# Values of one attention unit in a scratch tile, one unit fewer transposed on TensorE, and new leads

## The chip, the cores and the metric

The kernel runs on one core of a Trainium2 chip. The metric is the device time of one execution in microseconds (us). Times from several runs are given as their median; a profiled execution has a time of its own. The engines are TensorE (PE, matmuls, with its weight loads PEld), VectorE (DVE), ScalarE (ACT) and GpSimd (POOL). SyncE (SP) issues all DMAs of this kernel, in program order.

## The reference, cut to what matters

Attention for 4 batches, 8 heads, 576 tokens and head size 64. Heads 0 to 3 see the last 32 tokens ("local"), heads 4 to 7 see the tokens that are a multiple of 32 back ("strided"). Then two feed-forward networks over the 2304 tokens of width 512.

```
scores = where(mask, q @ k.T / 8, -1e9);  attn = softmax(scores);  x = attn @ v
x   = x / sqrt(mean(x*x) + 1e-6) * rms_g
x   = (silu(x @ w_gate) * (x @ w_val)) @ w_out          # 512 -> 1536 -> 512
out = relu(x @ w_in)**2 @ w_out2                        # 512 -> 2048 -> 512
```

All operands are float32, and each product is made of three matmuls of halves (high by high, high by low, low by high).

## The kernel before, in words

**Attention units.** A unit is a pair of heads of one batch; there are 16, in the order of pairs 0, 2, 1, 3 of each batch, so units 0 and 2 are local, 1 and 3 strided, and so on. A unit's steps are: load of q and k (`att_load` "qk", two buffers), scores on PE (`att_qk`, L464 and L476), the maximum (L507, scaled at L508), exponentials with sums on ACT (L524), the reciprocal (L538), the normalization (L545), a transpose of the probabilities, the product on values (`att_pv`, L612), a copy out (L646), and a sum of squares for the norm. The values have a load of their own (`att_load` "v", L439 and L443: one DMA of 384 KB, and for a local unit two more of 96 KB), into a pool of two buffers (`v_p`).

The transpose is done in one of two ways. Units below `NM` (L87, 7) use PE: `att_turn` (L567, small matmuls with an identity) into the two accumulator tiles `first_acc`, where their scores also lie, and `att_keep` copies them to SBUF (L579, ACT or DVE). The later units use a DVE transpose by blocks of 32 (`att_tr`, L553) and a copy of eight SBUF to SBUF DMAs (`att_swap`, L593). When unit `NM - 1` is kept, `done["acc"]` (L768) gives the accumulators' banks to the first output product of block 0. Both ways feed the same `att_pv`.

**Feed-forward.** The first half of network one runs over blocks of 512 tokens (the last has 256), six column tiles each (L1427 to L1429, three matmuls of one product). Block 0 needs the four units of batch 0; its norm is applied after the product, from a row kept in `norm0`, columns 0 to 511 of a scratch tile `fa`; its gates use columns 512 to 1535 (`tmp_slot`), and the weights' conversion uses columns from 1536. The weights come packed in pairs of matrices (1 MB, L1140) through two staging buffers and are converted on DVE, ACT and POOL (L1181 to L1222), as many steps as a unit of attention. The rest of network one and network two (L1912, L2318) are a scheme of seven products per eight.

**What sets the order.** A planner runs when the program is built: every piece of work is a task with a due time and steps; a step names its engine or engines, a cost, a condition and the times that it must wait for. `advance` (L357) takes, again and again, the engine that can start earliest, and on it the step with the smallest due time among those that can start within a small tolerance. So each engine's instructions stand in the planner's order, and an engine in the program never passes a waiting instruction by. The due time of an attention step is that of its unit less `PRI` of the step (the maximum: less `MXP`); the units of batch 0 are due at -50 + u, the others `ATT_LEAD` tiles before their block, the norm `PREP_LEAD` before it. `D_COST` is added to what a DVE step seems to end at before `D_BUSY` us. `PV_AHEAD` is how many units the scores may be ahead of the products on values. All loads wait for their buffer by `take` and `rel`; the values' load is a task of one step, due half a tile after its unit.

**Fillers.** While PE would be idle before block 0, `fill` (L2479) issues matmuls on a blank tile, whose results nobody reads.

Of the kernel before, what the change touches and what calls it, by code (L numbers as in the profile page):

```python
# [8 lines left out]
F32 = mybir.dt.float32  # L9
# [32 lines left out]
VW = LT * 2 * D  # L42
VM = LT // 2 * 2 * D
# [9 lines left out]
WST = 2  # L53

RING = 9

ATT_LEAD, ATT_STEP = 5.322, 0
PREP_LEAD = 6.258
W_LEAD = 0
X_LEAD = 4.164  # L60
WARM0 = 10

HOP = 0.15
# [12 lines left out]
N_QK, N_PV = {"loc": 160, "str": 96}, {"loc": 144, "str": 88}  # L76
QK0, PV0 = {"loc": 1.0, "str": 0.9}, {"loc": 1.25, "str": 0.9}

PRI = {"qk": -3.7, "mask": 12.1, "mx": -12.4, "exp": -0.1, "eps": -0.5, "sum": 15.6, "norm": -1.1, "turn": 3.4, "keep": 12.1, "tr": -1.6,
       "swap": -2, "pv": -2.7, "out": -1.4, "sq": -3, "ms0": 9.4, "add": -1.3}  # L80
MXP, LOADF, BIAS = 8.164, 0.752, 0.972

D_BUSY, D_COST, D_LATE, D_COST2 = 138.427, 1.084, 371.203, 0.648
PV_AHEAD = 5


NM = 7  # L87

ORDER0 = (0, 2, 1, 3)

# [17 lines left out]
    ("P1", 0, 0, "A", None), ("P5", 3, 1, "D", None), ("P6", 4, 2, "A", "s1"), ("P2", 1, 3, "C", "s1"),  # L108
    ("P7", 5, 4, "A", "u2"), ("P3", 6, 5, "D", "s5"), ("P4", 2, 6, "A", "c22"),
]  # L110
W2_LEAD, X2_LEAD, L2_LEAD = 9.789, -0.326, 6.418
X3_LEAD, O_LEAD, H_LEAD = 2.563, -0.69, -0.441
O_ORDER = [(0, 0), (0, 1), (1, 0), (1, 1), (0, 2), (1, 2), (0, 3), (1, 3)]
O_ORDER += [(3, 0)] + [(2, j) for j in range(4)] + [(3, j) for j in range(1, 4)]
O_ORDER += [(p, j) for p in range(4, 7) for j in range(4)]
W3_LEAD, LOADF2, BIAS2, TOL2 = 16.583, 0.334, 1.147, 0
X2_PRI = -1.337


def segments(t0, n):  # L120
# [107 lines left out]
def kernel(ctx: ExitStack, tc: tile.TileContext, loc, strd, w1, w2, g, cst, out):  # L228
# [13 lines left out]
    fa = qa[:, QKB * QKW:]  # L242
# [31 lines left out]
    v_p = pool("v", 2, early)  # L274
# [39 lines left out]
    rel = {k: deque([0.0] * caps[k]) for k in live}  # L314
    order = {}

    def room(k, n=1):
        return live[k] + n <= caps[k]

    def take(k):  # L320
        live[k] += 1
        return rel[k].popleft()

    def give(k, t):
        live[k] -= 1
        rel[k].append(t)

    def in_turn(kind, n):
        return order.get(kind, 0) == n
# [80 lines left out]
    first_acc, warming, ms0, first_in = [], [True], [], []  # L410

    def kind(u):
        return "loc" if units[u][1] < 2 else "str"
# [9 lines left out]
    def att_load(u, what):  # L423
        b, p = units[u]
        src = (loc if p < 2 else strd)[b, p % 2]
        w = QW[kind(u)] + KW[kind(u)]
        if what == "qk":
            o = QKW * turn_of("qk", QKB)
            t = qa[:, o:o + QKW]
            if p < 2:  # L430
                nc.sync.dma_start(out=t[:, :w], in_=src[:, :w])
            else:
                nc.sync.dma_start(
                    out=t[:, :2 * SL].rearrange("p (e c) -> p e c", e=2),
                    in_=src[:, :w].rearrange("p (e c) -> p e c", e=2)[:, :, :SL],
                )
        else:
            t = v_p.tile([128, VW + VM], F32, tag="v", name="v")
            nc.sync.dma_start(out=t[:, :VW], in_=src[:, w:w + VW])  # L439
            if p < 2:  # L440
                mid = src[32:96, w:w + VW].rearrange("p (k a n) -> p a k n", a=2, n=2 * D)
                for a in range(2):
                    nc.sync.dma_start(  # L443
                        out=t[64 * a:64 * a + 64, VW:].rearrange("p (k n) -> p k n", n=2 * D), in_=mid[:, a]
                    )
        qkv[what, u] = t
# [6 lines left out]
    def att_qk(u):  # L453
# [3 lines left out]
        masked = u < NM2  # L457
        if u < NM:
            sc = [first_acc[u % 2][:, h] for h in range(2)]
# [220 lines left out]
    def att_task(u, due):  # L680
# [5 lines left out]

        def load(what):
            def f(_, t):
                take(what)
                att_load(u, what)  # L690
                done[what, u] = lanes.dma(
                    QL[kd] + KL[kd] if what == "qk" else VW + (VM if kd == "loc" else 0), t,
                    3 if what == "v" and kd == "loc" else 1, 600,
                )
                turn("load" + what)
            return f
# [27 lines left out]
        def exp(i0, i1):  # L724
            def f(_, t):
# [3 lines left out]
                if NM <= u < NM2:  # L729
                    for h in range(2):  # L730
                        if i0 < nt * (h + 1) <= i1:
                            give("s", t)
            return (None, [[("A", 0.33 * (i1 - i0))]], f, None, due - PRI["exp"])

# [36 lines left out]
        def pv(_, t):  # L771
            take("s")
            take("s")
            att_pv(u)
            qkv.pop(("v", u))
            give("v", t)
            give("pt", t)
            turn("pv")

# [35 lines left out]
        def step(k, ok, alts, fn, when=None):  # L815
            return ok, alts, fn, when, due - PRI[k]

# [4 lines left out]
        if u < NM:  # L822
            steps += [
                (
                    lambda: in_turn("qk", u) and (u < 2 or ("sc", u - 2) in done), [[("T", QK0[kd] + 0.5, N_QK[kd] + 4)]], qk,
                    lambda: max(done["qk", u], done.get(("sc", u - 2), 5.3)), due - 10 - PRI["qk"],
                ),
# [53 lines left out]
        if not alone:  # L881
# [1 line left out]
            steps.append(step("add", None, [dvx(m)] if b == 0 else [dvx(m), gps(m)], add))  # L883
        tasks.append(Task(due, steps))
        tasks.append(Task(due + 0.5, [
            (lambda: room("v") and in_turn("loadv", u), [[("Q", 0.0)]], load("v"), lambda: rel["v"][0])
        ]))


# [225 lines left out]
    wst, wt, raws = {}, {}, []  # L1115
    slots_w = [None] * RING
    mats = [
# [1274 lines left out]
    for i in range(NB):  # L2392
        if i == 0:
            tasks.extend(split_tasks(
                (0, 0), -44, BLOCKS[0][1], lambda k: [(0, xr[0][:, k, 0:BLOCKS[0][1]])], got="xo"
            ))
        prep_task(i, at[0, i, 0] - PREP_LEAD if i else -45)
        if i >= LOADED:
            load_task(i, at[0, i, 0] - X_LEAD)
    for ph in NJS:  # L2400
# [63 lines left out]
    with tc.manual_schedule():  # L2464
# [19 lines left out]
        def next_load(due):  # L2484
# [4 lines left out]
            out=ms0[0], lhsT=blank[:, 0:1].to_broadcast([128, 128]), rhs=blank[:, 0:1].to_broadcast([128, 512]),  # L2489
# [113 lines left out]
```

## Time and profile before

| | us |
|---|---|
| runs of the kernel before (3) | 886.64, 888.31, 888.44; median 888.31 |
| profiled execution, its own time | 888.45 |
| its span, first to last instruction | 886.7 |
| around the span | 1.75 |
| PE busy | 873.9 (99%) |
| DVE busy | 651.2 (73%) |
| ACT busy | 443.7 (50%) |

The profile lists instructions with their start and duration from the span's first instruction. Matmuls are pipelined, so one that lasts 0.39 us can start 0.23 us after the one before; their records count every pass. A timeline row is start, duration, engine, line, operation, output<-input, shape, count, and in brackets the idle time of the engine before it with what ended it. "issue" is time in which the engine waited for nothing that the profile shows.

### The profile page before, as it was taken

To read this page: it belongs to the slowest core of one execution; us is meant where nothing else is said; L and a number is where in the kernel's file an instruction comes from. 1 tells how busy PE (TensorE), PEld (TensorE's weight loads), DVE (VectorE), ACT (ScalarE), POOL (GpSimd) and SP (SyncE) were. 2 spreads that over 40 slices of the span, in tenths; PEclk is the share of its full clock that TensorE was granted. 3 is DMA by queue.
4 is the path that set the end of the run, shared out by engine and by line. 5 is a ranking of instruction groups with operands and counts; after the bars stand their busy time and mean duration, and the time that the engine had idled before them with its cause. 6 is when DMAs were issued, how large, how long until landed. Compare 5 with 4: busy or idle time off the path is not lost.

```text
span 886.7 us, 17216 instructions
## 1 busy us (share of the span) xinstructions
PE 873.9 (99%) x6777; PEld 817.3 (92%) x6782; DVE 651.2 (73%) x1104; ACT 443.7 (50%) x1141; POOL 72.1 (8%) x66
## 2 busy tenths in 40 slices
PE   8999999999999999999999999999999999999998
PEld 5778778878888999999999999999999999999998
DVE  5998977978889776967965876868875456548466
ACT  5986866422312243434533556656565375364462
POOL 0210620100100000000100100001000003002002
PEclk9999999999999999999999999999999999999999
DMA  9865563676794995494498998876699989949714
GB/s 347 268 214 190 181 209 83 217 240 226 237 370 147 372 409 226 154 374 157 166 334 330 384 408 336 334 265 241 275 309 336 365 318 379 307 166 353 239 37 178
DMA packets 77586, 236.79 MB, mean 267 GB/s; under 512 B 7489, under 2 KB 29761, under 8 KB 71617
## 3 DMA queue, kind: packets, MB, share of 16 engines
q1 hardware_dynamic: 77504, 235.70, 73.4%
q8 instruction: 53, 0.87, 0.4%
q14 instruction: 29, 0.23, 0.1%
HBM read 151.91 MB, written 80.48 MB: 262 GB/s over the span
## 4 chain that ended last, share of the span: by engine, by line
PE 81%; DMA 10%; DVE 7%; issue 1%; ACT 1%; SPq 0%; DVEq 0%; ACTq 0%
PE a L1912 14%; PE pg L1912 7%; PE pb L1912 7%; PE gv L1427 6%; PE a L1427 5%; PE gv L1429 5%; PE a L1429 5%; PE a L1428 5%; PE gv L1428 5%; PE a L2318 5%; DMA wst_a<-in_w 5%; PE pg L2318 3%; DMA wi_d<-wst_a 2%; PE pb L2318 2%; DMA wf_d<-wst_a 2%; PE xo L612 1%
## 5 line engine op out<-in xcount | busy, mean ns | idle before, releaser
L1912 PE MATMUL a<-ra 128*128 128x384 f32 x912 | 173.4, 335 | 0.9 <-DVE fb L1960 0.6
L1912 PEld LDWEIGHTS a<-ra 128*128 128x128 f32 x912 | 159.7, 188 | 2.0 <-DVE fb L1960 0.9
L1427 PE MATMUL gv<-ra 128*128 128x512 f32 (+1 forms) x240 | 90.9, 379 | 0.0
L1429 PE MATMUL gv<-ra 128*128 128x512 f32 (+1 forms) x240 | 88.5, 369 | 0.1
L1428 PE MATMUL gv<-ra 128*128 128x512 f32 (+1 forms) x240 | 88.4, 369 | 0.0
L1912 PE MATMUL pg<-ra 128*128 128x384 f32 x426 | 83.6, 336 | 1.1 <-DVE fb L1960 1.0
L1912 PE MATMUL pb<-ra 128*128 128x384 f32 x426 | 83.0, 335 | 0.4 <-DVE fb L1960 0.4
L1912 PEld LDWEIGHTS pg<-ra 128*128 128x128 f32 x426 | 74.7, 188 | 2.1 <-DVE fb L1960 2.1
L1912 PEld LDWEIGHTS pb<-ra 128*128 128x128 f32 x426 | 74.8, 188 | 0.7 <-DVE fb L1960 0.7
L1366 DVE TENSOR_TENSOR wst_a<-fa,wst_a 128x512 fp32r<-128x512 f32 (+1 forms) x76 | 48.0, 633 | 22.0 <-ACT wst_a L1330 19.0
L1427 PEld LDWEIGHTS gv<-ra 128*128 128x128 f32 x240 | 45.2, 189 | 8.1 <-issue 0.3
L1429 PEld LDWEIGHTS gv<-ra 128*128 128x128 f32 x240 | 45.3, 189 | 7.8
L1428 PEld LDWEIGHTS gv<-ra 128*128 128x128 f32 x240 | 45.3, 189 | 6.9
L1330 ACT ACTIVATE wst_a<-fa 128x512 fp32r<-128x512 f32 (+1 forms) x59 | 33.9, 576 | 31.0 <-DMA wi_d<-wst_a 19.5
L1429 PE MATMUL a<-ra,rb 128*128 128x384 f32 x144 | 48.4, 336 | 0.0
L1427 PE MATMUL a<-ra,rb 128*128 128x384 f32 x144 | 48.4, 336 | 0.0
L1428 PE MATMUL a<-ra,rb 128*128 128x384 f32 x144 | 48.4, 336 | 0.0
L1427 PE MATMUL a<-ra 128*128 128x512 f32 (+1 forms) x120 | 45.6, 380 | 0.9 <-ACT pt L579 0.9
L1429 PE MATMUL a<-ra 128*128 128x512 f32 (+1 forms) x120 | 44.9, 375 | 0.0
L1428 PE MATMUL a<-ra 128*128 128x512 f32 (+1 forms) x120 | 44.8, 374 | 0.0
L1199 DVE SCALAR_TENSOR_TENSOR fa<-wst_a,fa 128x1024 int32<-128x1024 int32 x34 | 41.6, 1224 | 1.0
L1514 ACT ACTIVATE fa<-gv 128x512 f32<-128x512 f32 (+1 forms) x18 | 9.5, 527 | 65.4 <-PE gv L1429 65.4
(259 smaller groups left out, 1918.7 us busy)
## 6 DMA issues: line engine op xcount, KB each, us to landing
wst_a<-in_w SPq DMA_DIRECT2D x34, 1024.0 KB, 6.2
ra<-wi_d SPq DMA_DIRECT2D x18, 1792.0 KB, 10.6
wi_d<-wst_a SPq DMA_DIRECT2D x42, 512.0 KB, 4.0
rb<-wf_d SPq DMA_DIRECT2D x16, 1024.0 KB, 7.9
xf_d<-ra SPq DMA_DIRECT2D x21, 768.0 KB, 5.0
ra<-xf_d SPq DMA_DIRECT2D x21, 768.0 KB, 7.4
wo_d<-wst_a SPq DMA_DIRECT2D x14, 512.0 KB, 8.3
wf_d<-wst_a SPq DMA_DIRECT2D x28, 256.0 KB, 6.5
```

The lines of the kernel that those rows point to most:

```text
L612: nc.tensor.matmul(out=o, lhsT=v, rhs=rhs, start=True, stop=True)
L1199: nc.vector.scalar_tensor_tensor(out=bits(), in0=word(1), scalar=-0x40000000, in1=bits(), op0=ALU.bitwise_and, op1=ALU.bitwise_or)
L1330: nc.scalar.activation(out=dst, in_=by_form(raw(a, b)), func=ACTF.Copy)
L1366: eng.tensor_tensor(out=x[:, :, 1], in0=by_form(raw(a, b)), in1=x[:, :, 0].bitcast(F32), op=ALU.subtract)
L1427: nc.tensor.matmul(out=o, lhsT=whi, rhs=x_hi, start=first, stop=False)
L1428: nc.tensor.matmul(out=o, lhsT=whi, rhs=x_lo, start=False, stop=False)
L1429: nc.tensor.matmul(out=o, lhsT=wlo, rhs=x_hi, start=False, stop=last)
L1514: nc.scalar.activation(out=tile_t()[:, :n], in_=ps[:, :n], func=ACTF.Silu)
L1912: nc.tensor.matmul(out=o, lhsT=l, rhs=v, start=need is None and k + n == 0, stop=k == 1 and n == 2, skip_group_check=need is not None,)
L2318: nc.tensor.matmul(out=c[role, m]["ap"][:, :SN], lhsT=l, rhs=v, start=need is None and first and i == 0, stop=last and i == 2, skip_group_ ...
```

## The change

Unit 2 (the third) gets columns 0 to 1151 of the scratch tile `fa` for its values instead of a buffer of `v_p`; its load then has no buffer to wait for, and its product gives none back. `NM` goes from 7 to 6, so unit 6 is transposed by DVE and DMAs, and its scores go to the `s` banks. Leads, priorities and the planner's cost of DVE get other values, and `PV_AHEAD` goes from 5 to 6.

```diff
-ATT_LEAD, ATT_STEP = 5.322, 0
-PREP_LEAD = 6.258
+V_APART = 2
+
+ATT_LEAD, ATT_STEP = 5.891, 0.063
+PREP_LEAD = 7.496
 W_LEAD = 0
-X_LEAD = 4.164
+X_LEAD = 3.422
...
-PRI = {"qk": -3.7, "mask": 12.1, "mx": -12.4, "exp": -0.1, "eps": -0.5, "sum": 15.6, "norm": -1.1, "turn": 3.4, "keep": 12.1, "tr": -1.6,
-       "swap": -2, "pv": -2.7, "out": -1.4, "sq": -3, "ms0": 9.4, "add": -1.3}
-MXP, LOADF, BIAS = 8.164, 0.752, 0.972
-
-D_BUSY, D_COST, D_LATE, D_COST2 = 138.427, 1.084, 371.203, 0.648
-PV_AHEAD = 5
-
-
-NM = 7
+PRI = {"qk": -4.9, "mask": 15.2, "mx": -7.3, "exp": 0, "eps": -0.2, "sum": 10.8, "norm": -0.6, "turn": 2.2, "keep": 11.4, "tr": -3.1,
+       "swap": -4.1, "pv": -0.2, "out": 1.5, "sq": -4.8, "ms0": 10.3, "add": 0.4}
+MXP, LOADF, BIAS = 2.974, 0.752, 1.006
+
+D_BUSY, D_COST, D_LATE, D_COST2 = 143.605, 1.407, 343.785, 0.648
+PV_AHEAD = 6
+
+
+NM = 6
...
-W2_LEAD, X2_LEAD, L2_LEAD = 9.789, -0.326, 6.418
-X3_LEAD, O_LEAD, H_LEAD = 2.563, -0.69, -0.441
+W2_LEAD, X2_LEAD, L2_LEAD = 8.99, -0.326, 6.418
+X3_LEAD, O_LEAD, H_LEAD = 3.503, -1.055, -0.697
...
-W3_LEAD, LOADF2, BIAS2, TOL2 = 16.583, 0.334, 1.147, 0
-X2_PRI = -1.337
+W3_LEAD, LOADF2, BIAS2, TOL2 = 16.305, 0.334, 1.147, 0
+X2_PRI = -0.95
...
-            t = v_p.tile([128, VW + VM], F32, tag="v", name="v")
+            t = fa[:, 0:VW + VM] if u == V_APART else v_p.tile([128, VW + VM], F32, tag="v", name="v")
...
-                take(what)
+                if what == "qk" or u != V_APART:
+                    take(what)
...
-            give("v", t)
+            if u != V_APART:
+                give("v", t)
...
-            (lambda: room("v") and in_turn("loadv", u), [[("Q", 0.0)]], load("v"), lambda: rel["v"][0])
+            (
+                lambda: (u == V_APART or room("v")) and in_turn("loadv", u), [[("Q", 0.0)]], load("v"),
+                None if u == V_APART else lambda: rel["v"][0],
+            )
```

## Rows read from the trace of the kernel before

**Rows 1.** The page, part 1: busy time, share of the span, instructions.

```profile
PE 873.9 (99%) x6777; PEld 817.3 (92%) x6782; DVE 651.2 (73%) x1104; ACT 443.7 (50%) x1141; POOL 72.1 (8%) x66
```

**Rows 2.** Stretches: length, busy time by engine, granted PE clock, DMA share, GB/s.

```profile
0.00:20.00 20.00, 16.78 (x362) 10.06 (x366) 11.32 (x19) 10.79 (x52) 0.34 (x6) 1.00 0.94 343
20.00:40.00 20.00, 19.06 (x476) 15.10 (x474) 19.14 (x29) 18.89 (x84) 3.56 (x2) 0.91 0.84 273
...
80.00:280.00 200.00, 198.41 (x1810) 162.58 (x1797) 167.32 (x291) 88.68 (x305) 30.87 (x26) 0.99 0.64 214
280.00:880.00 600.00, 597.59 (x3488) 594.73 (x3488) 416.58 (x711) 293.79 (x584) 33.45 (x29) 1.00 0.77 286
```

**Rows 3.** Groups of PE by line, 0 to 75 us: the fillers.

```profile
L2479 PE MATMUL warm<-blank 128*128 128x512 bf16 x35 | 11.1, 475 | 1.6 <-DVE blank L2470 0.9 <-issue 0.7
...
L2479 PE MATMUL ms<-blank 128*128 128x512 bf16 x7 | 1.9, 381 | 0.2 <-issue 0.2
```

**Rows 4.** The chain of waits in order of time, 0 to 80 us.

```profile
9.70 9.46 DMA wst_a<-in_w
...
33.52 0.83 DVE nm L507
...
34.77 0.14 DVE ri L538
```

**Rows 5.** PE's waits over the whole span: total, times, longest.

```profile
PE xo L612 <- issue: 1.6, 1, 1.6
...
PE a L1427 <- ACT pt L579: 0.9, 1, 0.9
...
PE xo L612 <- DMA pt<-tr: 0.7, 2, 0.4
```

**Rows 6.** Timeline of PE: unit 2's product, unit 6's turn, the first output product.

```profile
30.34 1.54 PE L612 MATMUL xo<-pt,v 64*64 64x32 f32 x72
...
59.68 1.32 PE L567 MATMUL a<-cst_sb,sm 64*64 64x64 f32 x37
...
62.62 0.50 PE L1427 MATMUL a<-ra 128*128 128x512 f32 x1 [0.87 <-ACT pt L579]
```

**Rows 7.** Timelines of ACT and DVE: unit 5's copy, unit 6's normalization.

```profile
56.85 0.87 ACT L579 ACTIVATE pt<-a 128x384 f32<-128x384 f32 x2 [0.20 <-PE a L567]
...
58.48 0.83 DVE L545 TENSOR_TENSOR sm<-sm,ri 128x640 f32<-128x640 f32 x1
```

**Rows 8.** The tile of the later units' transposes, whole span: durations min/median/max in ns.

```profile
L593 SPq DMA_DIRECT2D pt<-tr x72: 507/590/1687, 83.5 to 205.7; - x72
L553 DVE STREAM_TRANSPOSE tr<-sm x9: 835/922/973, 82.5 to 181.2; 128x768 f32<-128x768 f32 x5, 128x640 f32<-128x640 f32 x4
...
DMA to landing us min/median/max: 1.8/2.7/9.5
```

**Rows 9.** Timeline of SP: the loads of the values of units 1 and 2.

```profile
5.23 0.45 SPq L439 DMA_DIRECT2D v<-in_strd  x1
...
20.12 0.34 SPq L439 DMA_DIRECT2D v<-in_loc  x1
```

**Rows 10.** Two stretches of the start, columns as in rows 2.

```profile
2.00:10.00 8.00, 7.84 (x146) 4.46 (x146) 2.04 (x4) 2.27 (x13) 0.00 (x0) 1.00 1.00 379
10.00:19.00 9.00, 7.57 (x203) 4.88 (x201) 8.76 (x15) 6.43 (x40) 0.00 (x0) 1.00 1.05 377
```

**Rows 11.** Timelines of SP and PE, 185 to 198 us: a late copy.

```profile
185.24 9.84 SPq L593 DMA_DIRECT2D pt<-tr  x8
...
194.53 0.39 PE L1429 MATMUL gv<-ra 128*128 128x512 f32 x1
...
197.54 0.50 PE L1427 MATMUL a<-ra 128*128 128x512 f32 x1
```

**Rows 12.** Two stretches behind it, columns as in rows 2.

```profile
195.00:200.00 5.00, 4.25 (x79) 3.54 (x80) 4.09 (x7) 1.62 (x6) 0.00 (x0) 0.80 0.73 170
200.00:205.00 5.00, 5.00 (x21) 4.06 (x20) 2.65 (x4) 0.50 (x2) 0.00 (x0) 0.86 0.78 274
```

## The prediction

> **What bounds the kernel now.** I read the busy line of the page first. TensorE (PE) is busy 99% of the span, VectorE (DVE) 73%, ScalarE (ACT) 50% [rows 1]: no other engine can bound the whole, so time goes only where PE stops, runs slowly, or does work that the result doesn't need. The table of stretches says where [rows 2]. From 80 to 880 us PE is idle 1.6 + 2.4 = 4.0 us out of 800. The first 20 us hold 3.2 idle us, the next 20 hold 0.9. So the feed-forward phases are a stream of matmuls at a fixed rate, and an edit to the attention's order can win little there.
>
> The start is another matter, and its busy digits mislead: the groups of the filler matmuls (on a blank tile, issued where PE would wait) hold 11.1 + 1.9 = 13.0 us [rows 3]. With the idle 4.1 us some 17 us of the first 41 are not work. In that stretch DVE is busy 19.1 us and ACT 18.9 of 20 [rows 2]: they, and the loads before them, set the moment at which block 0 streams. The chain of waits shows this: the load of the second weight pair (9.46 us until 19.16), then ACT and DVE one after the other on it, DVE's maximum of unit 4, the reciprocal of unit 3, and so on to PE [rows 4].
>
> Last, PE's waits past the start: 0.87 us before the first output product at 62.62, on ScalarE's copy of unit 6's turned probabilities, and 0.7 us on the late copy of a transposed tile near 195 [rows 5].
>
> **The sum is made against the profiled execution**: 888.45 us, its span 886.7 and 1.75 around it. That is 0.14 above the median of the runs, 888.31.
>
> **The change, part by part.**
>
> *Unit 6 leaves TensorE's transpose (NM 7 to 6).* Removed are its 40 small matmul records on PE: 37 in 1.32 us, the last three among the next product's [rows 6]. These lie in the in-order PE stream, so they go one for one: -1.3. Unit 6 also frees the accumulator banks: they now become free after unit 5's copy, at about 57.7 [rows 7], and the first output product has no copy to wait for. I let the 0.87 us go as well. Next in PE's order there is unit 5's product on values, right behind the turn, whose copy of 57.7 is long done; PE stays fed. Added: one DVE transpose of 128x640, 0.835 to 0.97 us, and a copy of eight DMAs, 0.51 to 0.59 us of SP each (4.1 to 4.7), landing 2.7 us later by the median, 9.5 at worst [rows 8]. Two ACT copies go in exchange, like unit 5's pair of 0.87 us [rows 7]. None of this is on PE; from 59.3, where unit 6's normalization ends [rows 7], 0.9 + 4.7 + 2.7 is 67.6, 5 us behind the first output product [rows 6], which is the cover: twelve such matmuls and those of block 0's next tile stand in PE's order there. If it fails, PE waits for the copy, by up to 6.8 us more with the worst landing. I take 0; the upper bound is the price of the one late copy that the trace has, +2.8 (worked out under B), the lower 0.
>
> *Unit 2's values go to the scratch tile.* Its step loses the only thing it waited for, the product of unit 0. Now SP issues it at 20.12, when that product is done [rows 9]. After the change its turn comes right behind the values of unit 1 (5.23) [rows 9], so its 576 KB (384 and twice 96) stand before the qk loads of units 2 and 3 and before the second weight pair (9.70 [rows 4]). At the 377 to 379 GB/s that DMA moved from 2 to 19 us, with all 16 engines busy, this is 589,824 / 378e3 = 1.6 us [rows 10]. The four loads behind it land up to 1.6 us later, and the second pair is on the chain [rows 4]. Against it: SP no longer stands before that load until 20.1, and 576 KB are gone from the stretch after 20. But unit 2's product ran at 30.34 [rows 6], 10 us after the load was issued, and PE's waits before products on values are on instruction issue and on late copies, on no load of values [rows 5]. So I see no direct gain in it. The columns are first reused for block 0's norm and gates, which stand behind all four products of the first batch on PE, unit 2's among them: no new wait. Values of units 3 and 4 may also be loaded one product earlier; neither was waited for. Bounds 0 to +1.6, taken +0.8: half, since DVE and ACT have attention work that can be put before the weights.
>
> The Trainium skill, "DMA: Bandwidth & Descriptors", section on queues, rings and completion order, says that each DMA engine consumes the descriptors of a ring in ring order. This speaks against moving a load forward on SP's one busy queue; the trace agrees in that the second weight load, with the loads issued before it still in flight, stood on the chain for 9.46 us [rows 4]. That page's specifications also limit HBM to about 358 GB/s for a core, by which the 576 KB would be 1.65 us and the term +0.83 in place of +0.8; the row is above that limit, and the row is used.
>
> *Priorities and leads.* The maximum's lead falls from 8.16 to 2.97. Today DVE does unit 4's maximum and its scaling at 33.52, before the reciprocal of unit 3 at 34.77, and the chain runs through both [rows 4]: behind it the maximum would cost unit 3 nothing, so the step wins 0 to 1.25 us. Taken: -0.8, nearer to the whole, since the chain has no other engine between the two. DVE work is made dearer in the first 143 us, attention and the block's preparation are due earlier, the second phase's weights later. These change which of several ready steps goes first on an in-order queue. No row prices them; the nearest are the single waits of about 0.8 us [rows 5]. Bounds: one such wait less or two more, -0.8 to +1.6; I take 0, since PE has 4.0 idle us in the 800 that follow and DVE is busy only 167 of 200 from 80 to 280 [rows 2], so that there is little to win and cover to lose.
>
> Sum: -1.3 - 0.87 + 0.8 - 0.8 = -2.2 us, so 886.3 in the profiled execution and **886.1** by the median.
>
> **Rivals.**
>
> *B: the late copy goes too.* At 185.24 the eight DMAs of one unit's transpose take 9.84 us on SP behind a weight store; its product on values then runs in pieces, from 194.9 to 197.5, 2.6 us where unit 2's took 1.54 [rows 6, 11], and the granted clock is 0.80 and 0.86 in the next two stretches of 5 us (part of them at 1.2 instead of 2.4 GHz): 1.1 + 5 x 0.34 = 2.8 us [rows 12]. The new leads move that unit against the store. If they meet no more and nothing like it comes, 886.1 - 2.8 = 883.3. For it: one of nine copies was hit, all others passed. Against: 10 copies now, with the same stores.
>
> *C: the start pays.* The value load delays the second weights by its full 1.6 us, and the maximum's move wins nothing (ACT is as full as DVE there, and would be next). Then -2.2 + 0.8 + 0.8 = -0.6, 887.7: no change that can be measured. By the Trainium skill's ring order (page and section as above) the delay would be whole.
>
> *D: slower, by late copies.* The place is SP's queue between 60 and 210 us, where each transposed unit issues eight DMAs in a row; earlier leads put them beside weight stores and loads. The price is the 2.8 us of the one seen. One more leaves +0.6; from two more on it decides: -2.2 + 5.6 = +3.4, 891.7. For it: there is one copy more, and SP took up to 9.84 us for eight [rows 11]. Against: 8 of 9 cost PE nothing.
>
> **How the numbers follow.** A measurement of this kernel tells about 0.2%, 1.8 us, from no change: faster is below 886.5, slower above 890.1. Forecast 0.36, B 0.21, C 0.25, D 0.18. The forecast stands just under the line, so of its 0.36 I count 0.26 as faster and 0.10 as the same; C is the same, but for 0.02 on either side; B is faster, with 0.01 left as the same; D is slower. Faster 0.48, same 0.32, slower 0.20. The likeliest case alone runs from 884.0, with its three open terms at their lower ends, to 887.7, where it becomes C. The range takes in B with 0.8 us below it, and of D the case of a single late copy beside a start that pays (886.1 + 2.8 + 1.6 = 890.5): 882.5 to 890.5.
>
> **What would show it.** Right: six units' turns on PE, the last near 55, and no wait on the copy before the first output product, which comes some 2 us before 62.62; ten transposes on DVE. The value load of unit 2 on SP before 8 us; the second weights landing between 19.2 and 20.8; the reciprocal of unit 3 no longer behind unit 4's maximum; fillers and idle of the first 41 us still near 17. Busy PE down by 1.3 us less what the fillers change. Wrong: fillers shorter or longer by over 2 us (the start then decides, not unit 6); a new wait of PE on a copy or on DVE between 60 and 280 with a granted clock below 1; or the wait at 195 gone, which would make it B.

## The result, and the profile after

The change makes the kernel slower: median 893.87 us (892.89 to 894.71, 4 runs) against 887.66 for the kernel before on the same chip (886.64 to 888.44, 4 runs), a ratio of 1.0061 with a 95% interval of 1.0042 to 1.0079. Timed again (the run "after_again" below), it was 894.62 against 888.21 (1.0078, 1.0063 to 1.0093). The forecast was 886.1 and its range ended at 890.5: its sign was wrong, and the time lies outside the range. The profiled execution took 894.71, its span 892.9. Its busy times, to set beside [rows 1]:

```profile
PE 874.6 (98%) x6736; PEld 818.9 (92%) x6741; DVE 652.0 (73%) x1097; ACT 444.4 (50%) x1141; POOL 80.6 (9%) x72
```

TensorE's busy time is the same to 0.7 us, and 41 records are gone: the 40 of unit 6's turn, as forecast, and one filler (a matmul on the blank tile). So the 6 us are time in which PE waits, or runs at the lower clock. Stretches of the changed kernel, to set beside [rows 2, 10, 12]:

```profile
20.00:40.00 20.00, 15.61 (x384) 12.41 (x381) 14.46 (x22) 14.88 (x67) 0.00 (x0) 0.75 0.73 246
20.00:25.00 5.00, 1.17 (x32) 1.04 (x28) 2.88 (x5) 2.35 (x15) 0.00 (x0) 0.50 0.82 323
...
80.00:280.00 200.00, 197.06 (x1885) 161.47 (x1884) 167.32 (x283) 90.10 (x318) 33.85 (x29) 0.98 0.64 217
105.00:110.00 5.00, 3.19 (x94) 2.66 (x93) 5.00 (x8) 4.02 (x18) 2.10 (x1) 0.84 0.25 95
110.00:115.00 5.00, 4.97 (x17) 4.42 (x18) 4.29 (x9) 5.00 (x27) 3.61 (x4) 0.50 0.95 344
205.00:210.00 5.00, 3.89 (x82) 3.35 (x82) 3.53 (x6) 1.63 (x6) 0.00 (x0) 1.00 0.71 172
```

From 20 to 40 us PE is busy 15.6 us and was busy 19.1; from 80 to 280 it idles 2.9 us and idled 1.6. Two holes stand out, one at 20 to 25, one at 105 to 115, each with a granted clock down to 0.50 (1.2 in place of 2.4 GHz) behind or in it. The late copy of [rows 11] is still there, 10 us later: its eight DMAs again take 10 us on SP, and the product runs in pieces from 205.4 to 208.0. Only the clock stays at 1.00 behind it, where the kernel before had 0.80 and 0.86 [rows 12]. SP, then PE:

```profile
195.26 10.20 SPq L594 DMA_DIRECT2D pt<-tr  x8
...
205.44 0.30 PE L613 MATMUL xo<-pt,v 64*64 64x32 f32 x4 [0.41 <-DMA pt<-tr]
```

PE's waits name the holes (beside [rows 5]):

```profile
PE xo L613 <- issue: 3.8, 1, 3.8
PE a L477 <- DMA fa<-in_loc: 1.7, 1, 1.7
PE a L1433 <- ACT pt L580: 1.5, 1, 1.5
PE xo L613 <- DMA pt<-tr: 1.1, 3, 0.4
PE bc L928 <- POOL inv L919: 1.0, 1, 1.0
...
PE sc L477 <- DVE inv L912: 0.8, 1, 0.8
```

To see when the time is lost I followed the n-th matmul of the feed-forward through the records of both kernels, and summed PE's gaps and the fillers (matmuls on the blank tile) up to it:

| n-th feed-forward matmul | before: start, gaps + fillers | after | after_again |
|---|---|---|---|
| 4th (block 0 starts) | 41.12, 16.4 | 45.45, 20.2 | 44.57, 19.5 |
| 97th | 76.52, 17.4 | 81.53, 22.4 | 80.68, 21.7 |
| 253rd | 124.75, 18.1 | 134.88, 24.2 | 133.38, 24.9 |
| 541st (all attention done) | 204.72, 18.9 | 213.50, 25.3 | 212.10, 26.0 |
| 4356th, the last | 882.67, 21.3 | 889.00, 26.3 | 888.05, 27.4 |

Some 3.5 to 4.3 us are lost before block 0 starts, another 4.5 or 3.9 by the 541st, and 2.0 to 2.4 come back after it (PE's gaps there are 1.4 and 1.0 us shorter in all than before). At the 97th the two kernels have not done the same work: unit 6's product on values (1.25 us) stands at 65.59 in the kernel before and at 84.35, behind the 97th, in the changed one. At the other four marks the products are level. For equal work the changed kernel loses 1.9 (in after_again 2.0) us from the 4th to the 97th, 3.9 (3.2) from there to the 253rd, and wins back 1.3 from there to the 541st. The first of these stretches holds a longer wait for a copy (1.53 us for 0.87) and a granted clock of 0.66 from 50 to 55 us; no experiment takes it apart.

**The first hole.** The loads on SP, changed kernel (start, duration, line):

```profile
5.67 0.44 SPq L440 DMA_DIRECT2D v<-in_strd  x1
6.16 0.44 SPq L440 DMA_DIRECT2D fa<-in_loc  x1
7.53 3.19 SPq L444 DMA_DIRECT2D fa<-in_loc  x2
11.74 0.33 SPq L432 DMA_DIRECT2D fa<-in_loc  x1
...
13.17 2.87 SPq L1146 DMA_DIRECT2D wst_a<-in_w  x2
```

and in the kernel before:

```profile
7.48 0.33 SPq L431 DMA_DIRECT2D fa<-in_loc  x1
8.92 0.38 SPq L433 DMA_DIRECT2D fa<-in_strd  x1
9.70 6.22 SPq L1140 DMA_DIRECT2D wst_a<-in_w  x2
```

Unit 2's values (L440 and L444 into `fa`) stand where the forecast put them, but unit 2's q and k go out at 11.74 and not at 7.48, the second weight pair at 13.17 and not at 9.70: 3.5 to 4.3 us later, where the forecast said 1.6 at most. SP itself waits:

```profile
SPq L444 <- DMA wst_a<-in_w: 2.0, 1, 2.0
```

The DMA records carry eight completion semaphores in turn, and a DMA's record waits until the one eight places before it has landed. The first weight pair is fourth on SP, so the twelfth DMA waits for its landing (at 10.09; the twelfth is issued at 10.11); the change makes the last of unit 2's three DMAs the twelfth, and all that follows stands behind it. Now the chain of waits (beside [rows 4]) runs through these loads:

```profile
2.63 9.02 DMA v<-in_loc
11.74 6.13 DMA fa<-in_loc
...
18.95 1.29 PE xo L613 x64
20.23 3.83 issue
24.06 0.44 PE xo L613 x8
```

PE gets unit 2's scores at 17.91, 1.9 us later than before, and then stops for 3.83 us in the middle of unit 0's product, where nothing that the profile shows is awaited. Before, the same place cost 1.6 [rows 5]. In this pause lies a block of 16 KB on a DMA queue of kind "instruction". The DMA queues, 17 to 18 us of the kernel before:

```profile
q8 instruction: 1, 0.02, 6.8%
```

and 21 to 22 us of the changed kernel:

```profile
q8 instruction: 1, 0.02, 6.9%
```

I read this as PE waiting for its own code; no run moved the code to try it. By the records that packet starts 0.3 us behind the product before the change (17.25 against 16.97) and 2.7 us after it (21.60 against 18.88), and in all eighteen traces PE goes on 2.3 to 2.8 us after the packet starts. The Trainium skill, "Runtime: NRT & Kernel Launch", section on instruction fetch mechanics, says that code is refilled in blocks of 16 KiB and that the cost is mostly hidden; the trace agrees on the size, and on "mostly": of the eight such packets in the first 60 us of the changed kernel seven go with no such pause. The eighth costs 3.8 us on PE's path, and 1.6 before the change.

**The second hole.** PE, changed kernel, at block 1's norm:

```profile
105.62 1.17 PE L906 MATMUL msb<-ones,ssq 128*128 128x1 f32 x10
...
107.81 1.18 PE L477 MATMUL sc<-fa 64*32 64x64 f32 x78 [0.79 <-DVE inv L912]
110.03 2.36 PE L928 MATMUL bc<-cst_sb,inv 128*128 128x64 f32 x10 [1.05 <-POOL inv L919]
```

DVE and then POOL in the same stretch:

```profile
101.12 1.64 DVE L1540 TENSOR_TENSOR ra<-fa,ra 128x512 fp32r<-128x512 f32 x1
...
105.86 1.22 DVE L1205 SCALAR_TENSOR_TENSOR fa<-wst_a,fa 128x1024 int32<-128x1024 int32 x1
...
107.60 0.15 DVE L912 TENSOR_SCALAR inv<-msb 128x5 f32<-128x5 f32 x1
107.67 1.21 DVE L1210 SCALAR_TENSOR_TENSOR fa<-wst_a,fa 128x1024 int32<-128x1024 int32 x1
```

```profile
100.69 1.52 POOL L546 TENSOR_TENSOR sm<-sm,ri 128x640 f32<-128x640 f32 x1 [2.21 <-DVE ri L539]
107.83 2.10 POOL L919 TENSOR_TENSOR inv<-inv,half 128x5 f32<-128x5 f32 x1 [5.62 <-DVE inv L912]
```

The row sums are ready at 106.8, but DVE is full (busy 5.00 of 5) and does the norm step only at 107.60; POOL's power takes 2.10 us. DVE's L1540 takes 1.64 us where its like takes 0.69, beside a POOL instruction.

### The profile page after: what moved, and what is told of

Same layout as the page of the kernel before. It is cut to its first block, busy times and chain, and to the rows that moved or that the text cites. A ratio compares the mean times of both kernels' runs of the same rounds, so it can differ in the third digit from the quotient of the medians.

```text
span 892.9 us, 17136 instructions
## 1 busy us (share of the span) xinstructions
PE 874.6 (98%) x6736; PEld 818.9 (92%) x6741; DVE 652.0 (73%) x1097; ACT 444.4 (50%) x1141; POOL 80.6 (9%) x72
## 4 chain that ended last, share of the span: by engine, by line
PE 88%; DVE 5%; DMA 5%; issue 1%; SPq 1%; ACT 0%; POOL 0%; DVEq 0%; ACTq 0%
PE a L1918 16%; PE pg L1918 9%; PE pb L1918 8%; PE a L2324 7%; PE a L1433 6%; PE a L1435 6%; PE a L1434 6%; PE gv L1433 5%; PE gv L1435 5%; PE gv L1434 5%; PE pb L2324 2%; PE pg L2324 2%; PE pb L1435 2%; PE pb L1433 2%; PE pb L1434 2%; PE pg L1435 2%
## 5 line engine op out<-in xcount | busy, mean ns | idle before, releaser
L1918 PE MATMUL a<-ra 128*128 128x384 f32 x858 | 160.4, 335 | 0.3 <-ACT a L1955 0.3
L1918 PEld LDWEIGHTS a<-ra 128*128 128x128 f32 x858 | 150.1, 188 | 0.9 <-ACT a L1955 0.6
L1918 PE MATMUL pg<-ra 128*128 128x384 f32 x480 | 94.1, 336 | 0.7 <-DVE fb L1966 0.7
L1918 PEld LDWEIGHTS pg<-ra 128*128 128x128 f32 x480 | 84.4, 188 | 1.1 <-DVE fb L1966 1.0
L1372 DVE TENSOR_TENSOR wst_a<-fa,wst_a 128x512 fp32r<-128x512 f32 (+1 forms) x76 | 48.0, 633 | 19.2 <-ACT wst_a L1336 16.4
L1336 ACT ACTIVATE wst_a<-fa 128x512 fp32r<-128x512 f32 (+1 forms) x55 | 31.7, 577 | 33.3 <-DMA wi_d<-wst_a 21.1
L1205 DVE SCALAR_TENSOR_TENSOR fa<-wst_a,fa 128x1024 int32<-128x1024 int32 x34 | 42.7, 1256 | 0.9
L1210 DVE SCALAR_TENSOR_TENSOR fa<-wst_a,fa 128x1024 int32<-128x1024 int32 x34 | 42.5, 1250 | 0.7
```

The source lines that it names most:

```text
L1205: nc.vector.scalar_tensor_tensor(out=bits(), in0=word(1), scalar=-0x40000000, in1=bits(), op0=ALU.bitwise_and, op1=ALU.bitwise_or)
L1210: nc.vector.scalar_tensor_tensor(out=bits(), in0=word(0), scalar=29, in1=bits(), op0=ALU.logical_shift_right, op1=ALU.bitwise_or)
L1336: nc.scalar.activation(out=dst, in_=by_form(raw(a, b)), func=ACTF.Copy)
L1372: eng.tensor_tensor(out=x[:, :, 1], in0=by_form(raw(a, b)), in1=x[:, :, 0].bitcast(F32), op=ALU.subtract)
L1918: nc.tensor.matmul(out=o, lhsT=l, rhs=v, start=need is None and k + n == 0, stop=k == 1 and n == 2, skip_group_check=need is not None,)
```

## The experiments

Ratios are against the kernel before on the same chip, with 95% intervals. Where nothing else is said, every engine's order but for the edited instructions is that of the kernel named.

**1. after_defer**: the changed kernel, unit 2's three value DMAs behind the third weight load.

```diff
+            if u == V_APART:
+                held.append(issue)
+            else:
+                issue()
...
+        if n == 2:
+            held.pop()()
```

> The changed kernel with one thing moved: the three DMAs of unit 2's values stand on SP behind the third weight load instead of ahead of the loads of units 2 and 3 (every other instruction keeps its place on its engine). Theory S (the early values load delays the start: in the changed kernel the q and k load of unit 2 left SP at 11.74 instead of 7.48 and the second weights landed at 22.0 instead of 19.2): the start comes back, 886 to 889 us, q and k of unit 2 issued near 7.5, no stall of 3.8 us on issue in the first product on values. Theory L (the new leads and priorities give the engines a worse order): it stays at 892 to 895 us, whatever SP does.

Measured: 892.48, ratio 1.0042 (1.0018 to 1.0066). Unit 2's q and k go out at 7.45, the second weights at 9.54, PE's pause shrinks from 3.8 to 1.9 us; the 97th feed-forward matmul starts at 76.65, 0.13 behind the kernel before where the changed kernel was 5.0 behind (in both of these unit 6's product is still to come). Block 0 starts 2.2 us later than before, since a second pause of that kind, 1.8 us, comes at 30.9. From the 97th to the 253rd matmul 3.1 us are lost for equal work all the same. So the rows of the start are as theory S said, and the time, not told apart from that of the changed kernel, lies in theory L's range: the start is one loss, and the second hole another that doesn't hang on it.

**2. before_early**: the kernel before, its plan untouched, unit 2's values in the scratch tile and issued behind unit 1's.

```diff
+            if u == 1:
+                b2, p2 = units[2]
+                v_issue(fa[:, 0:VW + VM], loc[b2, p2 % 2], QW["loc"] + KW["loc"], p2)
```

> The kernel before with its plan unchanged on every engine; only unit 2's values go to the scratch tile, and their three DMAs stand on SP right behind the values of unit 1. Theory S: the whole loss appears without any new lead, 892 to 895 us, and q and k of unit 2 leave SP near 11.7. Theory L: the load costs at most its bytes, 0 to 1.6 us, so 887.5 to 889.5 us.

Measured: 891.91, ratio 1.0032 (1.0011 to 1.0053). The move alone makes the kernel before slower by about 2.8 us: unit 2's q and k at 12.36, a pause for code of 4.0 us, block 0 starts 4.4 us later, and granted clock 0.66 and 0.65 from 20 to 30 us. This is the changed kernel's first loss without its leads; in the time it lies between the two theories.

**3. before_nm6, after_no_apart, before_leads**: one part alone, or all but one, planned anew: six units on PE (an edit to the kernel before); all but the scratch tile; all new constants with seven units and no scratch tile (both edits to the changed kernel).

```diff
-NM = 7
+NM = 6
```

```diff
-V_APART = 2
+V_APART = -1
```

```diff
-V_APART = 2
+V_APART = -1
...
-NM = 6
+NM = 7
```

> The kernel before with NM 6 alone, planned anew with the old leads. The prediction's first step (unit 6's turn and the wait on its copy gone, 2.2 us) says 885.0 to 886.5 us. Its rival, that the order around it changes and gives the gain back in new waits of PE, says 887 to 890 us. Neither S nor L touches this run.

> The changed kernel with unit 2's values back in the ring of two buffers (V_APART -1), planned anew with the new leads and NM 6. Theory S: 885 to 889 us, since the start's loads are as before and the turn of unit 6 is saved. Theory L: 892 us or more.

> The leads and priorities alone: the kernel before with all new constants, seven units on TensorE and unit 2's values in the ring. The prediction's reading (the constants only choose among ready steps): -0.8 to +1.6 us against the kernel before. Rival: a set of constants fits one plan only, as the other parts alone showed (+2.6% for six units, +4.45% without the scratch tile): more than 1% slower, by waits on weights and on DVE between 60 and 280 us.

Measured: before_nm6 1.0261 (1.0240 to 1.0282), after_no_apart 1.0445 (1.0421 to 1.0470), before_leads 1.0185 (1.0160 to 1.0209). PE's longest wait in each of the three, in this order:

```profile
PE a L2318 <- DMA rb<-wf_d: 15.2, 1, 15.2
```

```profile
PE pg L2324 <- DMA rb<-wf_d: 15.8, 1, 15.8
```

```profile
PE a L568 <- DVE sm L546: 4.1, 3, 3.0
```

In before_nm6 the first output product stands at 60.48, 2.14 us ahead of the 62.62 of [rows 6] (what that is made of is told below). Then the planner's order comes out differently, and a weight tile is waited for by 15.2 us, until 752; before_leads waits 4.1 us on unit normalizations. Neither the forecast's first step nor its rival foresaw before_nm6, nor did theory S after_no_apart; before_leads is over 1% slower, as its rival said. Each part without the others is far worse than all together. So, in this planner, the parts have no prices that could be added: the constants fit one plan.

**4. before_3tiny and before_1big**: what delays SP, the number of DMAs or their bytes? The kernel before with three DMAs of 1 KB, or one of 576 KB, behind unit 1's values.

```diff
+            if u == 1:
+                for k in range(3):
+                    nc.sync.dma_start(out=fa[:, 2 * k:2 * k + 2], in_=src[:, 2 * k:2 * k + 2])
```

```diff
+            if u == 1:
+                nc.sync.dma_start(out=fa[:, 0:VW + VM], in_=src[:, 0:VW + VM])
```

> The kernel before with three DMAs of 1 KB each behind unit 1's values on SP, where the changed kernel has unit 2's values (576 KB in three DMAs). Theory 1, SP holds only a fixed number of loads in flight, so the number of DMAs delays what stands behind them: unit 2's q and k are issued at 10 to 12 us in place of 7.5, and the kernel is 1.5 to 4 us slower. Theory 2, the bytes delay it: unit 2's q and k stay within 0.5 us of 7.5 and the time within 0.8 us of the kernel before.

> The kernel before with one DMA of 576 KB behind unit 1's values on SP, into columns that nothing uses then. Theory 1 (number of DMAs in flight): unit 2's q and k are issued less than 1.5 us later than 7.5, and the kernel is 0.5 to 2 us slower (the bytes alone, 1.6 us at 378 GB/s). Theory 2 (bytes): the second weight pair lands 1.6 us later than 19.16 or more, and the kernel is as slow as the one with unit 2's values early, +2.8 us.

Measured: before_3tiny 890.02, ratio 1.0013 (0.9999 to 1.0027); before_1big 890.19, ratio 1.0026 (1.0016 to 1.0035). SP in the first:

```profile
6.17 4.82 SPq L448 DMA_DIRECT2D fa<-in_strd  x3
12.20 0.33 SPq L431 DMA_DIRECT2D fa<-in_loc  x1
...
13.06 3.53 SPq L1143 DMA_DIRECT2D wst_a<-in_w  x2
```

and in the second:

```profile
7.51 0.33 SPq L431 DMA_DIRECT2D fa<-in_loc  x1
...
11.06 4.87 SPq L1142 DMA_DIRECT2D wst_a<-in_w  x2
```

Three DMAs that carry 3 KB delay SP as much as the 576 KB did (12.20 and 13.06, in before_early 12.36 and 13.23): the number of DMAs in flight delays the issues, with next to no bytes. But one large DMA, which leaves unit 2's issue at 7.5, lands the second weights 1.7 us later (20.84), as theory 2 said, and loses as much by the start of block 0: +3.5 us, and +2.9 with the tiny ones. Its q and k are waited for by 0.7 us only, and then PE's pause for code is 4.1 us, where the tiny ones' is 3.0. So both theories are half right: the number of DMAs and the bytes each delay the loads, and each time the pause for code is longer too. It doesn't add up: both together (before_early) cost 4.4 us there. In the whole time the tiny DMAs are not told apart from none, and theory 1's 1.5 us or more did not come.

**5. before_g_late and after_defer_g**: one DMA fewer ahead, the 2 KB of `g_sb` behind the third weight load; on the kernel before, and on after_defer.

```diff
-        nc.sync.dma_start(out=g_sb, in_=g)
         while tasks:
...
+        if n == 2:
+            nc.sync.dma_start(out=g_sb, in_=g)
```

> The kernel before with one DMA fewer ahead of unit 2's q and k: the 2 KB load of the norm's factors (g_sb, first used near 58 us) stands behind the third weight load on SP. Theory 1, SP issues a DMA when the one eight places before it has landed: unit 2's q and k go out near 5.7 us and not at 7.5, unit 3's at 7.5, the second weight pair near 8.9 and not at 9.7, and the time is 0 to 1.5 us shorter than that of the kernel before. Theory 2, SP only follows what is done otherwise (bytes, buffers): the issues stay within 0.3 us of those of the kernel before, and so does the time.

> The same move on top of the first repair of the changed kernel. Theory 1: the second weight pair goes out near 8.9 us and not at 9.5, first feed-forward product up to 0.8 us earlier, 0 to 1.5 us faster than the first repair alone. Theory 2: the same as the first repair alone, to 0.5 us.

Measured: before_g_late 888.35, ratio 0.9996 (0.9982 to 1.0010), no change; after_defer_g 891.10, ratio 1.0015 (1.0000 to 1.0029). Unit 2's q and k go out at 6.7, not 5.7, unit 3's at 8.9 as before, the second weights at 9.3: what holds them there, and in the kernel before, is the q and k buffer that PE's scores of units 0 and 1 give back (they end at 6.7 and 8.9 in this trace); only the weights stood on the place in flight. So theory 1 holds for one of three issues, and is worth nothing in the time: taking a place away wins nothing here, adding some costs. With both repairs of the start the changed kernel's interval (to 1.0029) ends below where that of the unrepaired one begins (1.0042 and 1.0063): the start is shown to be a cause, and by the medians the larger part of the loss. Whether the small load adds to the first repair is not resolved.

**6. after_again and after_inv_first**: the changed kernel again, and with one DVE instruction (L1205 at 105.86) moved behind the norm step.

```diff
+            if n == HOLD_BITS:
+                held_bits.append(issue)
+            else:
+                issue()
```

> The changed kernel itself, timed beside the next three on the same chip. Both theories: within 0.1% of its earlier ratio to the kernel before, 1.0061.

> One DVE instruction of the weights' conversion (the bits step, 1.22 us at 105.86) is moved behind the second block's norm step (inv) that it stands ahead of. Theory 1, the second loss of the changed kernel is this chain (row sums, inv on DVE, its power on POOL, the row product on PE): inv starts 1.2 us earlier, PE's 0.8 us wait on inv shrinks to under 0.3, the granted clock near 107 to 116 stays above 0.8 where it was 0.69 and 0.63, and the kernel is 2 to 4 us faster than the changed one. Theory 2, the chain is late anyway because POOL's power step takes 2.10 us there: the wait of 1.05 us on POOL stays, the clock falls as before, and the gain is 0 to 0.8 us.

Measured: 1.0078 (1.0063 to 1.0093) and 1.0075 (1.0056 to 1.0094), no gain. The wait on the norm step is gone, and in its place:

```profile
PE bc L932 <- DVE sm L492: 2.5, 1, 2.5
```

The size is theory 2's, the wait another: what DVE now does later is waited for instead. In after_again the granted clock stayed at 1.00 through that hole, where it was 0.69 and 0.63 in the first profile, and yet the 97th to the 541st matmul took 131.4 us, against 132.0. So this loss comes without the lower clock too. How much of the first profile's loss the clock is stays open, since after_again has a pause for code of 1.0 us at 125.5 that the first profile lacks.

**7. after_bc_late, after_defer_bc, before_bc_late**: PE's row products (bc) behind the next twelve matmuls.

```diff
+        if i == 1:
+            held_bc.append(issue)
...
+                if held_bc:
+                    held_bc.pop()()
```

> The changed kernel with one group of matmuls moved on TensorE: the second block's row products (bc, 10 matmuls) stand behind the next twelve matmuls of the feed-forward and not ahead of them. Theory 1, the second loss is TensorE's place in that chain: the wait of 1.0 to 1.2 us on POOL goes, the 0.8 to 1.0 us on DVE stays, and the kernel is 1 to 2.5 us faster than the changed one. Theory 2, DVE is full in that stretch (busy 9.9 of 10 us) and what TensorE waits for only moves: another wait of 0.8 us or more turns up within 15 us behind it, and the gain is under 0.5 us.

> Both repairs in the changed kernel: unit 2's three value loads behind the third weight load on SP, and the row products behind the next twelve matmuls. If the start and this chain are the two main losses, each worth what it showed alone (2.9 and 1 to 2.5 us), it is 4 to 5.5 us faster than the changed kernel, that is 0 to 2 us slower than the kernel before. If the losses overlap, or the time turns up elsewhere, it is no better than the first repair alone, 3 us or more slower than the kernel before.

> The kernel before with the same one group of matmuls moved. There its wait is 0.75 us, on DVE. If TensorE's place is what counts, it is 0.5 to 0.8 us faster than the kernel before; if DVE is the bound there, the same to 0.1%, since the row's use on DVE comes 1.5 us later.

Measured: 1.0098 (1.0075 to 1.0121), 1.0065 (1.0041 to 1.0088) and 1.0016 (1.0000 to 1.0032): better in none, and the medians are higher. In after_bc_late PE no longer waits for POOL, but for the next weights' conversion, and later for the use of the row products:

```profile
PE gv L1441 <- ACT ra L1228: 1.1, 1, 1.1
...
PE sc L477 <- DVE xr L953: 1.0, 1, 1.0
```

So theory 2 holds, for this move: DVE and what hangs on it are late there, and PE waits for one of them or for another.

**8. after_less_pool and after_defer_less**: four POOL instructions between 87 and 102 us given to ACT as plain copies; three low halves of weights and the division of unit 8's probabilities are left out by it.

```diff
+                if parts[0][0] == "P" and n in ACT_LO:
+                    nc.scalar.activation(out=w[:, 1], in_=cell["r"][:, e], func=ACTF.Copy)
...
+        if u in ACT_NORM:
+            nc.scalar.activation(out=sm[:, :n], in_=sm[:, :n], func=ACTF.Copy)
+            return
```

> The changed kernel with four POOL instructions between 87 and 102 us given to ACT as plain copies: three halves of the weights' low parts, and unit 8's normalization, so that these low parts and that division are left out of the result. All DVE, TensorE and SP orders stay. Theory 1, POOL holds DVE up: of the DVE instructions that run beside these four, three take 1.67, 1.23 and 1.64 us where their like take 0.69; they fall to 0.69, the norm step on DVE comes about 2.4 us earlier, TensorE's waits on DVE and on POOL near 106 to 110 (together 2.2 us) shrink to under 1 us, and the kernel is 1.5 to 3 us faster than the changed one. Theory 2, DVE there waits for TensorE's products and ACT's copies anyway: the three durations fall, but idle time of DVE takes their place, and the gain is under 0.5 us.

> The same on top of the first repair (unit 2's three value loads behind the third weight load); the low parts of three halves and unit 8's division are left out here too. If the start and DVE held up by POOL are the two main losses, 4 to 6 us faster than the changed kernel, within 1.5 us of the kernel before. If the second loss has another cause, no better than the first repair alone, 3 us or more slower than the kernel before.

Measured: after_less_pool 1.0070 (1.0052 to 1.0087), after_defer_less 890.06, 1.0026 (1.0008 to 1.0044). DVE in the first:

```profile
89.67 0.69 DVE L1547 TENSOR_TENSOR ra<-fa,ra 128x512 fp32r<-128x512 f32 x1
...
97.49 0.70 DVE L1193 TENSOR_SCALAR fa<-wst_a 128x1024 int32<-128x1024 int32 x1 [1.52 <-DMA wst_a<-in_w]
...
100.87 0.69 DVE L1547 TENSOR_TENSOR ra<-fa,ra 128x512 fp32r<-128x512 f32 x1
```

The three durations fall to 0.69 or 0.70, as both theories said, and PE's wait on the norm step (0.8 to 1.0) is gone. But POOL's power still takes 2.09 and is waited for by 1.2 us, and DVE now waits 1.5 us for a weight load. From the 97th to the 253rd matmul after_less_pool needs 51.8 us, after_again 52.7, and after_defer_less 51.9 against 52.6 of after_defer: 0.8 to 0.9 us, between the theories, and below what the whole time can resolve. The size is rough: these stretches hold pauses for code of 1.0 to 1.5 us, but for after_defer's, and there the granted clock is 0.66 from 105 to 110 us. POOL holding DVE up is a part of the second loss, not all of it.

## Why the prediction was wrong

**"Unit 2's values go to the scratch tile" (+0.8, bounds 0 to +1.6): this step failed.** Its place and sign were right: SP issues the load right behind unit 1's, and the second weights and the q and k behind it come late. It was sized by the bytes over the measured rate. In the changed kernel the second weights land at 22.0 (21.4 in after_again), not at 20.8 or before, and block 0 starts 3.5 to 4.3 us later; in before_early, the move alone, 4.4 at that point and 2.8 in the time. Two terms were missing: the places in flight (three DMAs, not 576 KB, push SP's next issues behind the landing of the first weights; before_3tiny shows it), and the pause for code, which stood in [rows 5] as "issue 1.6" and which I read as a constant. It isn't: 1.6 became 3.0 to 4.2 in each kernel that put something there, and was 1.9 to 2.7 where the load was put back. The argument for the cover, that PE is not waiting for any load of values, was true and beside the point, since what came late was q and k, a load that stood behind them.

**"Unit 6 leaves TensorE's transpose" (-1.3 and -0.87): the second term failed too.** The turn's 40 records are gone. But the wait of 0.87 did not go: with six units under the old leads (before_nm6) it is 1.02, in the changed kernel 1.53. That before_nm6 has its first output product 2.14 us earlier, near the 2.2 worked out, is luck: 1.3 of it is the turn, and most of the rest is unit 5's product (0.92 us), which stands behind that point there and before it in the kernel before. PE in before_nm6:

```profile
60.48 0.50 PE L1427 MATMUL a<-ra 128*128 128x512 f32 x1 [1.02 <-ACT pt L579]
```

PE and then ACT in the changed kernel, and ACT in the kernel before:

```profile
60.70 1.61 PE L568 MATMUL a<-cst_sb,sm 64*64 64x64 f32 x48
...
65.19 1.25 PE L613 MATMUL xo<-pt,v 64*64 64x32 f32 x72
67.98 0.50 PE L1433 MATMUL a<-ra 128*128 128x512 f32 x1 [1.53 <-ACT pt L580]
```

```profile
66.54 0.49 ACT L580 ACTIVATE pt<-a 128x384 f32<-128x384 f32 x1 [2.52 <-PE xo L613]
```

```profile
61.81 0.77 ACT L579 ACTIVATE pt<-a 128x320 f32<-128x320 f32 x2 [0.67 <-PE xo L612]
```

Unit 5's turn ends at 62.3, but its copy starts at 66.54, when unit 4's product has given back the buffer of turned probabilities; the kernels have one (`PTB` is 1). In the kernel before, unit 6's copy waited in the same way for unit 5's product. So the wait passed from unit 6 to unit 5. I took the copy's time of 57.7 from the old order, in which unit 4's product stood earlier (50.76); with six units it stands right ahead of the first output product, under the old leads (58.21) and the new. That the copy waits for this buffer is read from these rows and the kernel, not tried.

**"Priorities and leads" (0, bounds -0.8 to +1.6): the wrong kind of term.** The leads alone cost 1.85%, six units alone 2.6%, and both together without the scratch tile 4.45%. In the changed kernel's plan what is left of them is the second hole: PE's gaps grow by 1.4 us more than before from the 97th to the 541st matmul (2.8 in after_again, 1.0 of it the pause at 125.5). Some 0.8 us of the loss there is POOL holding up DVE; the rest lies between DVE being full, POOL's power and the weights' loads, and no run parts it further. Counted for equal work the stretch to the 253rd loses 3.2 to 3.9 us, twice the bound of two waits of 0.8; and the term stood alone, with a range as if it could be had without the others. Of the maximum's -0.8 nothing shows: in the chain after, a maximum at 37.21 and its scaling still stand directly ahead of a reciprocal at 38.24.

**The rivals.** C (the start pays) was the right place at half the size or less. D had the right side and the wrong place: copies of turned tiles are waited for by 1.1 us in all, against 0.7. B's late copy did not go; it moved to 205. The 1.3 us that the changed kernel wins back from the 433rd to the 541st matmul (28.7 us for 30.1) go with the lower clock that followed the copy in the one trace of the kernel before. The copy needn't bring it: before_g_late and before_bc_late keep the late copy, at clock 1.00, and take 28.4 and 28.5 us. So 1.7 of the 2.8 us in B's and D's price was the clock of one execution. Of the signs, "fillers and idle still near 17" failed: gaps and fillers up to block 0 grew by 3.1 to 3.8 us, all of it idle time, as the fillers didn't grow. The last turn ended at 62.3, not near 55. And a new wait on DVE with a clock below 1 came, at 107.

No version tried here is faster than the kernel before; before_g_late equals it.

## What to carry to other kernels

Price a DMA that is put ahead on a full queue by what stands behind it: by its bytes, by the places in flight that it takes (here three small ones cost nearly as much as one large by the start of block 0), and by what the first late consumer delays in turn. A pause that the profile calls "issue" is not a constant: where it lies behind a loaded queue, ask what it will be when the load moves. Where a planner makes the order, the parts of a change can't be priced and added; hold the plan fixed and move single instructions if you want to know what one of them costs. A wait on a buffer's chain may pass to the next unit when its owner goes: look at what that unit's copy waits for. And compare marks in two traces only where both have done the same work.

## What was not expected of the hardware

- TensorE pauses where it seems to wait for its own code: 1.4 to 4.2 us at one place in the program, 64 matmuls into unit 0's product, ending 2.3 to 2.8 us after a packet of 16 KB on the instruction queue starts, and 1.0 to 1.8 us elsewhere in some traces (at 30.9 in after_defer, at 125.5 in after_again). What decides when that packet starts, from 0.0 to 2.8 us after the product began, stays open.
- Some DVE instructions that run beside one of POOL take 0.6 to 1.1 us more: 1.64 where 0.69 is usual. In the changed kernel with the first repair eight DVE instructions before 210 us lie over 0.3 us above the median of their like, and all eight overlap one on POOL (three of three in the kernel before); some sixty others that overlap one are not. The Trainium skill, "SBUF — State Buffer", section on the two separate sides, calls the port pair that DVE and GpSimd share an exclusive lock, held for the whole instruction, with the loser blocked. The trace agrees for these: when the POOL instructions were taken away, three that had taken 1.67, 1.23 and 1.64 us in after_again took 0.69 or 0.70.
- POOL's power of 128x5 elements took 2.10 us with a DVE instruction started beside it, and 1.19 at the same step of the kernel before, where DVE paused for 0.42 us as it began. The same lock from the other side would do that; it was not tried.
- The granted clock behind nearly equal waits (0.8 and 1.0 us; 1.0 and 1.2) differs from one execution to the next: 0.69 and 0.63 in one profile of the changed kernel from 106.5 to 116.5 us, 1.00 in the other.
